# Attention and spectral layers in one program: exponents and scores take five banks in turn, the first projections are stored from other buffers, and a chunk's stack is loaded by eight transfers instead of twelve

## The chip, the cores and the metric

One core of a Trainium2 chip runs the whole program. The metric is the device time of one execution in microseconds (us). TensorE (PE in the profile) multiplies matrices and writes to PSUM, which has eight banks of 512 float32 a partition; its weight loads have a row of their own, PEld. VectorE is DVE, ScalarE is ACT, GpSimd is POOL, and SP issues most transfers between the chip's memory (SBUF) and HBM. Each engine works through its own list of instructions in order, and waits where an instruction needs what another engine has not yet done.

## The reference

Four layers in a row, A, B, A, B, over x of 2048 positions by 576. Each adds to x what it makes of its normalised x:

```python
qkv = (x @ wqkv).reshape(B, S, 3, H, Dh)          # H = 32 heads of Dh = 18
scores = einsum("bhqd,bhkd->bhqk", q, k) * Dh ** -0.5
mask = (i - j >= 0) & (i - j < 256)                # a sliding window
o = softmax(where(mask, scores, -1e9)) @ v         # layer A
x = x + o @ wo
x = x + irfft2(rfft2(_layernorm(x)) * W)           # layer B
```

## The kernel before

The program runs `layer_a` and `layer_b` twice. Only the second half of `layer_a` is touched: the attention.

*Numbers in two parts.* A matmul takes operands in a short float format, so most operands are split into a high part and a low part, and a product is summed from three. `proj(i, c, tag, halves)` makes unit i (128 of the 1152 rows of q and k) for chunk c (512 positions) in 14 such steps. With `halves` each step is two matmuls of 64 rows that may run at once, into two banks; ScalarE copies one bank (L747), VectorE adds the other (L748), GpSimd makes the high part and the low part (L749, L750), and SP stores both to `qk_d` in HBM (L755). The result stands in a tile `sg`, of which there are two. Units 0 and 1 come ahead of the loop, and units 2 to 8 are spread over it by the table `goal`, step by step.

*Stacks.* For a group n of four heads, `stack_load(n, c)` brings q and k of a chunk from `qk_d` to SBUF: head pairs `hp` lie in partitions from 64 * hp on, and there three slots of 18 rows hold high or low parts, so that one matmul sums the three products. Each slot is one transfer: 2 tensors x 2 head pairs x 3 slots, 12 a chunk.

*The loop.* t runs from -10 to 129. Block x of 128 positions belongs to group x // 16. In turn t the program does, for pair 0 and then for pair 1: two exponent blocks `exps(t, pair, hp)` (a matmul E on TensorE, L822, then the exponent on ScalarE, L823, into a tile `P`, of which there are five), then two score maxima `score_max(t + 10, pair, hp)` (a matmul S, L790, and the masked maximum on VectorE, L792, into `m`), and after pair 0 the products with v, `pv(t - 2)` (U, L842). Then come the projection steps of the turn; in turns before t = 2 the first half of them stands after pair 0. So the maxima run ten turns ahead of the exponents; for t < 0 there are only maxima and projections, and from t = 118 on only exponents. Every fourth turn `m_rows` turns four blocks' maxima around (tpm, L798) and sends them as a row of q (L805), and `norm` turns results around (tpo, L852) and divides them (L855, L857). GpSimd masks the exponents (L825, L828).

*Banks.* U has one of eight, `pj` two. `S` has three, which maxima, `m_rows` and `norm` use in turn. `E` has two, which the four exponent blocks of a turn use in turn (and units of i = 2 with odd c before the loop reaches t = 0). In the last turns some exponents use banks of S. A matmul into a bank waits until the reader of its former content is done: ScalarE for exponents, VectorE for maxima.

The order on every engine is the order of the code: nothing is rearranged by a scheduler. The numbers in names such as `E37_1` are the turn and the head.

## Time and profile before

| | us |
|---|---|
| median of 3 runs | 1580.11 (1578.26 to 1594.03) |
| the profiled execution | 1586.13 |
| its span, first to last instruction | 1584.4 |
| TensorE busy | 1452.4 (92%) |
| VectorE busy | 944.0 (60%) |
| ScalarE busy | 823.8 (52%) |
| GpSimd busy | 753.4 (48%) |
| mean granted TensorE clock | 0.964 of full speed |

The attention loop of the first layer A runs from about 107 us (first S) to 505 us, with its first exponent (t = 0) at 139 us; that of the second from about 900 to 1300 us. In rows of waits the columns are the engine and line that waited, what released it, the total of us, how many times, and the longest. In rows of groups, a line, engine and operation come first, then "busy, mean ns of one", and behind the bar the idle time ahead of it and what ended it. A matmul's recorded time runs from its start to its modelled end, so matmuls overlap in the rows, and the distance of two starts says more than one duration.

### The profile page before, as it was taken

How to read it: one execution, taken by the hardware profiler on the slowest of the kernel's cores; microseconds unless marked ns; L12 is line 12 of the kernel's file. 1: busy time of each engine (PE TensorE's matmuls, PEld its weight loads, DVE VectorE, ACT ScalarE, POOL GpSimd, SP SyncE). 2: the span in 40 equal slices, each digit the busy share in tenths (PEclk: the TensorE clock that was granted, in tenths of full speed). 3: DMA queues.
4: the chain of work that ended last, by engine and by line, in shares of the span. 5: the costliest groups of instructions: out<-in, count | busy, mean ns of one | idle time of the engine just before them, and what ended most of it. 6: DMA issues, size and time to landing. Idle time of an engine off the chain costs nothing. (4 is left out here: it accounts for less than half of the span.)

```text
span 1584.4 us, 35203 instructions
## 1 busy us (share of the span) xinstructions
PE 1452.4 (92%) x12312; PEld 1077.3 (68%) x12312; DVE 944.0 (60%) x3083; ACT 823.8 (52%) x1900; POOL 753.4 (48%) x1240
## 2 busy tenths in 40 slices
PE   7998999999999899877879989999999998997787
PEld 7976666666655799536779766666666557995376
DVE  4337777777764555444543377777777645554445
ACT  5524666666667344224445246666666673442244
POOL 2185556555545333144611855555555463332445
PEclk9999999999988999988989999999999899999889
DMA  6656455554444366666474564544444443657664
GB/s 205 177 182 207 142 156 183 152 165 145 151 128 123 118 196 200 220 195 209 142 229 118 181 202 146 155 150 145 139 130 149 128 129 118 196 194 230 191 206 139
DMA packets 196414, 264.43 MB, mean 167 GB/s; under 512 B 87182, under 2 KB 109326, under 8 KB 195406
## 3 DMA queue, kind: packets, MB, share of 16 engines
q1 hardware_dynamic: 184494, 243.28, 49.6%
q10 hardware_dynamic: 10976, 15.59, 3.0%
q0 software_dynamic: 768, 3.31, 0.8%
q8 instruction: 99, 1.62, 0.4%
q14 instruction: 77, 0.63, 0.1%
HBM read 163.46 MB, written 100.91 MB: 167 GB/s over the span
## 5 line engine op out<-in xcount | busy, mean ns | idle before, releaser
L792 DVE CUSTOM_DVE_ANT_0 jk<-S,mask 128x384 bf16<-128x384 f32 (+2 forms) x1024 | 499.5, 529 | 144.3 <-PE S L790 130.8
L823 ACT ACTIVATE P<-E 128x384 f32<-128x384 f32 (+2 forms) x1024 | 427.8, 473 | 204.3 <-PE E L822 176.6
L825 POOL TENSOR_SCALAR_AFFINE_SELECT P<-P 128x512 f32<-128x512 f32 x256 | 163.0, 637 | 311.0 <-ACT P L823 292.0
L822 PE MATMUL E<-qs,ks 64*128 64x384 f32 (+2 forms) x1024 | 285.2, 429 | 10.2 <-ACT P L823 8.2
L790 PE MATMUL S<-ks,qs 63*128 63x384 f32 (+2 forms) x1024 | 250.7, 362 | 9.4 <-DVE m L792 9.0
L822 PEld LDWEIGHTS E<-qs,ks 64*128 64x128 f32 x1024 | 138.3, 186 | 136.4 <-ACT P L823 80.7
L842 PE MATMUL U<-P,vq 128*19 128x128 f32 (+1 forms) x3840 | 208.2, 336 | 0.3
L741 PE MATMUL pj<-xh,wqh 64*128 64x512 f32 (+1 forms) x640 | 172.5, 404 | 5.5 <-ACT sg L747 3.4
L790 PEld LDWEIGHTS S<-ks,qs 63*128 63x128 f32 x1024 | 141.9, 190 | 27.0 <-DVE m L792 20.5
L842 PEld LDWEIGHTS U<-P,vq 128*19 128x19 f32 x3840 | 91.2, 99 | 100.5 <-issue 40.8
L828 POOL TENSOR_SCALAR_AFFINE_SELECT P<-P 128x512 f32<-128x512 f32 x224 | 142.7, 637 | 0.0
L741 PE MATMUL pj<-xl,wqh 64*128 64x512 f32 (+1 forms) x512 | 136.1, 395 | 0.0
L741 PE MATMUL pj<-xh,wql 64*128 64x512 f32 (+1 forms) x640 | 129.2, 398 | 1.4 <-POOL wql L431 1.4
L527 PE MATMUL ops<-oroom 128*128 128x288 f32 x784 | 112.4, 299 | 4.4 <-DVE oroom L510 3.0
L527 PEld LDWEIGHTS ops<-oroom 128*128 128x128 f32 x784 | 105.2, 188 | 6.2 <-DVE oroom L510 4.0
L741 PEld LDWEIGHTS pj<-xh,wqh 64*128 64x128 f32 (+1 forms) x640 | 95.0, 187 | 11.2 <-ACT sg L747 3.9
L171 POOL TENSOR_TENSOR eo<-xn 128x287 f32<-128x287 f32 x32 | 26.1, 817 | 150.4 <-ACT xn L169 150.4
L741 PEld LDWEIGHTS pj<-xh,wql 64*128 64x128 f32 (+1 forms) x640 | 84.4, 190 | 6.9 <-POOL wql L431 2.0
L792 DVE DVE_READ_ACCUMULATOR2_ANT m<- 128x1 f32 x1024 | 85.0, 83 | 0.0
L199 PE MATMUL pf<-dc,et 128*128 128x290 f32 x384 | 72.3, 313 | 9.7 <-DVE et L190 6.5
L741 PEld LDWEIGHTS pj<-xl,wqh 64*128 64x128 f32 (+1 forms) x512 | 78.6, 187 | 3.0
L750 POOL TENSOR_TENSOR sg<-sg 128x512 fp32r<-128x512 f32 x56 | 72.2, 1289 | 4.7
(179 smaller groups left out, 2567.0 us busy)
## 6 DMA issues: line engine op xcount, KB each, us to landing
qk_d<-sg SPq DMA_DIRECT2D x56, 512.0 KB
qs<-qk_d SPq DMA_DIRECT2D x384, 72.0 KB
ks<-qk_d SPq DMA_DIRECT2D x384, 72.0 KB
v_d<-vt SPq DMA_DIRECT2D x32, 304.0 KB
vq<-v_d SPq DMA_DIRECT2D x16, 608.0 KB
yd<-ye SPq DMA_DIRECT2D x32, 290.0 KB
wt<-in_w SPq DMA_DIRECT2D x16, 580.0 KB
x<-ofree SPq DMA_DIRECT2D x32, 288.0 KB
```

What stands on the lines that cost most here:

```text
L171: P.tensor_add(eo[:, 0, 1:288], xn[:, 1:288], xn[:, 575:288:-1])
L199: T.matmul(o, et[:, c, si], m(5 * c + mi), start=q == 0, stop=False)
L527: self.nc.tensor.matmul(self.ps[u][n][:, 0:288], x, self.w[p][:, wk * D + n * 288:wk * D + n * 288 + 288], start=first and i == 0, stop=la ...
L741: T.matmul(ps, w[r, wk], xT(xk, cs)[r], start=s == 0, stop=s == len(ks) - 1)
L750: P.tensor_sub(sg[:, 1], su, sg[:, 0].bitcast(F32))
L790: T.matmul(ps[:, 0:N], q[b:b + 63, pair, i * 128:i * 128 + 128], k[b:b + 63, pair, lo:hi], start=True, stop=True)
L792: V.tensor_tensor_reduce(out=jk[:, 0:N], in0=ps[:, 0:N], in1=mask[:, 384 - N:384], scale=1.0, scalar=-3e38, op0=ALU.add, op1=ALU.max, accu ...
L822: T.matmul(ps[:, 0:nq], k[b:b + 64, pair, j * 128:j * 128 + 128], q[b:b + 64, pair, j * 128:j * 128 + nq], start=True, stop=True)
L823: A.activation(p[:, hl_, 0:nq], ps[:, 0:nq], AF.Exp, scale=SC)
L825: P.affine_select(out=p[:, :, 0:128], in_=p[:, :, 0:128], pattern=[[0, 4], [1, 128]], compare_op=ALU.is_ge, fill=0.0, base=0, channel_mult ...
L828: P.affine_select(out=p[:, :, 256:384], in_=p[:, :, 256:384], pattern=[[0, 4], [-1, 128]], compare_op=ALU.is_gt, fill=0.0, base=0, channel ...
L842: T.matmul(U[32 * h:32 * h + 19, (q0 % 4) * 128:(q0 % 4) * 128 + 128 * (q1 - q0)], vts[n][:, j, h], pt[n, j][:, h, (q0 - j) * 128:(q1 - j) ...
```

## The change

It has four parts.

1. `bank(name)` hands out five banks in a fixed order, S S E E S, one place further with each call once t is 0 or more; all users of S and E in the loop call it: maxima, exponents, `m_rows`, `norm`. For t < 0 it always gives a bank of S. What was a separate rule for the last turns' exponents goes.
2. A unit with `halves` that ends while t < 0 puts its result into a buffer of `P` (five, unused before t = 0), not into one of the two `sg`.
3. For such a unit ScalarE's copy stays in place, but VectorE's sum, GpSimd's split and the store are kept in a list `later`, and done after the next two maxima.
4. `qk_cols` lays the columns of the weights so that the two heads of a pair alternate row by row in `qk_d`. A slot of 18 partitions by 2 heads is then one run of 36 rows, and one transfer can bring two neighbouring slots: 8 transfers a chunk in place of 12, with the same bytes.

On TensorE the order of instructions is the same, and what some wait for is another. Turn 37, first before, then after (E37_0 to E37_3 are exponents, S47 the maxima of block 47, U the products with v; Activation is ScalarE, Pool is GpSimd):

```order
L822 MATMUL E37_0_3688<-qs0_1034,ks0_1035 128x384 [waits Activation_49]
L822 MATMUL E37_2_3691<-qs0_1034,ks0_1035 128x384 [waits Activation_49]
L790 MATMUL S47_0_0_3694<-ks0_1035,qs0_1034 128x384 [waits DVE_49]
L790 MATMUL S47_0_1_3698<-ks0_1035,qs0_1034 128x384 [waits DVE_49]
L842 MATMUL U_1038<-P2_2_3520,vq2_2748 19x256 [waits Pool_49]
L842 MATMUL U_1038<-P2_2_3520,vq2_2748 19x256 x3
L842 MATMUL U_1038<-P2_3_3570,vq2_2748 19x128 [waits Pool_49]
L842 MATMUL U_1038<-P2_3_3570,vq2_2748 19x128 x3
L822 MATMUL E37_1_3712<-qs0_1034,ks0_1035 128x384 [waits Activation_49]
L822 MATMUL E37_3_3715<-qs0_1034,ks0_1035 128x384 [waits Activation_49]
L790 MATMUL S47_1_0_3720<-ks0_1035,qs0_1034 128x384 [waits DVE_49]
L790 MATMUL S47_1_1_3724<-ks0_1035,qs0_1034 128x384 [waits DVE_49]
```

```order
L831 MATMUL E37_0_3628<-qs0_1034,ks0_1035 128x384 [waits DVE_49]
L831 MATMUL E37_2_3631<-qs0_1034,ks0_1035 128x384 [waits Activation_49]
L799 MATMUL S47_0_0_3634<-ks0_1035,qs0_1034 128x384 [waits Activation_49]
L799 MATMUL S47_0_1_3638<-ks0_1035,qs0_1034 128x384 [waits DVE_49]
L851 MATMUL U_1038<-P2_2_3464,vq2_2704 19x256 [waits Pool_49]
L851 MATMUL U_1038<-P2_2_3464,vq2_2704 19x256 x3
L851 MATMUL U_1038<-P2_3_3514,vq2_2704 19x128 [waits Pool_49]
L851 MATMUL U_1038<-P2_3_3514,vq2_2704 19x128 x3
L831 MATMUL E37_1_3652<-qs0_1034,ks0_1035 128x384 [waits DVE_49]
L831 MATMUL E37_3_3655<-qs0_1034,ks0_1035 128x384 [waits Activation_49]
L799 MATMUL S47_1_0_3660<-ks0_1035,qs0_1034 128x384 [waits Activation_49]
L799 MATMUL S47_1_1_3664<-ks0_1035,qs0_1034 128x384 [waits DVE_49]
```

The first of each pair of exponents now waits for a maximum on VectorE, and the first of each pair of scores for an exponent on ScalarE.

On VectorE, ahead of t = 0, the sum of a unit moves behind two maxima. Unit 2, chunk 1, in the turn of block 3, before and after (`jk` with `m` is a maximum, the row of `m` alone its second half, `sg2_1` the sum, `jk4` the next block):

```order
L792 ISA jk3_0_1_1393,m0_0_1268<-S3_0_1_1391,mask_1026 128x384
L792 ISA m0_0_1268 128x1
L748 TENSOR_TENSOR sg2_1_1403<-sg2_1_1403,pj2_1_1_1338 128x512
L792 ISA jk3_1_0_1411,m0_0_1268<-S3_1_0_1409,mask_1026 128x384
L792 ISA m0_0_1268 128x1
L792 ISA jk3_1_1_1415,m0_0_1268<-S3_1_1_1413,mask_1026 128x384
```

```order
L801 ISA jk3_0_1_1377,m0_0_1256<-S3_0_1_1375,mask_1026 128x384
L801 ISA m0_0_1256 128x1
L801 ISA jk3_1_0_1391,m0_0_1256<-S3_1_0_1389,mask_1026 128x384
L801 ISA m0_0_1256 128x1
L801 ISA jk3_1_1_1395,m0_0_1256<-S3_1_1_1393,mask_1026 128x384
L801 ISA m0_0_1256 128x1
L751 TENSOR_TENSOR sg2_1_1387<-sg2_1_1387,pj2_1_1_1322 128x512
```

Five units in each layer A move so; on ScalarE and GpSimd the order stays. On SP each chunk's twelve loads become eight, and the first unit's store, which stood between two chunks' loads, comes after them.

```diff
@@ qk_cols
             for hp in range(2):
-                for pair in range(2):
-                    h = head_of(n, hp, pair)
-                    c += [qk * D + h * DH + d for d in range(DH)]
+                c += [qk * D + head_of(n, hp, pair) * DH + d for d in range(DH) for pair in range(2)]
@@ proj
-                        sg = wp.tile([128, 2, 512], F32R, tag="sg", name=f"sg{i}_{c}", bufs=2)
-                        if halves:
-                            su = sg[:, 1].bitcast(F32)
-                            A.copy(su, ps[0])
-                            V.tensor_add(su, su, ps[1])
-                            P.tensor_copy(sg[:, 0], su)
-                            P.tensor_sub(sg[:, 1], su, sg[:, 0].bitcast(F32))
+                        if halves and t < 0:
+                            sg = wp.tile([128, 4, 384], F32, tag="P", name=f"sg{i}_{c}", bufs=5).rearrange("p a b -> p (a b)")[:, 0:1024].bitcast(F32R).rearrange("p (a t) -> p a t", a=2)
                         else:
-                            A.copy(sg[:, 0], ps[0])
-                            V.tensor_sub(sg[:, 1], ps[0], sg[:, 0].bitcast(F32))
-
-                        (nc.scalar if i < 2 else nc.sync).dma_start(qk_d[:, 128 * i:128 * i + 128, cs].rearrange("a r t -> r a t").bitcast(F32), sg.bitcast(F32))
+                            sg = wp.tile([128, 2, 512], F32R, tag="sg", name=f"sg{i}_{c}", bufs=2)
+                        su = sg[:, 1].bitcast(F32) if halves else ps[0]
+                        A.copy(su if halves else sg[:, 0], ps[0])
+
+                        def rest():
+                            if halves:
+                                V.tensor_add(su, su, ps[1])
+                                P.tensor_copy(sg[:, 0], su)
+                            (P if halves else V).tensor_sub(sg[:, 1], su, sg[:, 0].bitcast(F32))
+                            (nc.scalar if i < 2 else nc.sync).dma_start(qk_d[:, 128 * i:128 * i + 128, cs].rearrange("a r t -> r a t").bitcast(F32), sg.bitcast(F32))
+                        if halves and t < 0:
+                            later.append(rest)
+                        else:
+                            rest()
+            turns, later = [0], []
+
+            def bank(name):
+                turns[0] += t >= 0
+                return pp.tile([128, 512], F32, name=name, **(dict(tag="E", bufs=2) if turns[0] % 5 > 2 else dict(tag="S", bufs=3)))
@@ stack_load
-                for which, t, parts in ((0, q, (0, 0, 1)), (1, k, (0, 1, 0))):
+                for which, t, parts in ((0, q, ((0, slice(0, 1)), (1, slice(0, 2)))), (1, k, ((0, slice(0, 2)), (2, slice(0, 1))))):
                     for hp in range(2):
                         r0 = 144 * n + 72 * which + 36 * hp
-                        for slot, part in enumerate(parts):
+                        for slot, part in parts:
                             b = 64 * hp + 18 * slot
-                            nc.sync.dma_start(t[b:b + 18, :, cs].bitcast(F32),
-                                              qk_d[part, r0:r0 + 36, cs].rearrange("(f d) t -> d f t", f=2).bitcast(F32))
+                            nc.sync.dma_start(t[b:b + 18 * (part.stop - part.start), :, cs].bitcast(F32), qk_d[part, r0:r0 + 36, cs].bitcast(F32))
@@ score_max, m_rows, exps, norm
-                ps = pp.tile([128, 512], F32, tag="S", name=f"S{x}_{pair}_{hp}", bufs=3)
+                ps = bank(f"S{x}_{pair}_{hp}")
-                tp = pp.tile([128, 4, 128], F32, tag="S", name=f"tpm{n}_{c}", bufs=3)
+                tp = bank(f"tpm{n}_{c}").rearrange("p (a t) -> p a t", a=4)
-                ps = pp.tile([128, 512], F32, name=f"E{x}_{hl_}", **(dict(tag="S", bufs=3) if pair and NX - LEAD <= x < NX - 4 else dict(tag="E", bufs=2)))
+                ps = bank(f"E{x}_{hl_}")
-                tp = pp.tile([128, 4, 128], F32, tag="S", name=f"tpo{n}_{c}", bufs=3)
+                tp = bank(f"tpo{n}_{c}").rearrange("p (a t) -> p a t", a=4)
@@ the loop
                         if t + LEAD < NX:
                             score_max(t + LEAD, pair, hp)
+                    while later:
+                        later.pop()()
                     if pair == 0 and 0 <= t - 2 < NX:
                         pv(t - 2)
```

## The prediction

> **What bounds the kernel now.** I read the page's first part, then stretches of the span with their granted clock, then the list of waits, and at last the timeline of one turn.
>
> ```profile
> span 1584.4 us, 35203 instructions
> PE 1452.4 (92%) x12312; PEld 1077.3 (68%) x12312; DVE 944.0 (60%) x3083; ACT 823.8 (52%) x1900; POOL 753.4 (48%) x1240
> 160.00:440.00 280.00, 279.00 (x2861) 176.05 (x2857) 213.84 (x823) 185.70 (x449) 159.09 (x236) 1.00 0.51 155
> 487.00:505.00 18.00, 16.61 (x179) 8.51 (x179) 4.86 (x18) 15.73 (x38) 11.18 (x17) 1.00 0.39 114
> 126.50:130.00 3.50, 3.50 (x20) 3.44 (x18) 1.91 (x9) 0.00 (x0) 0.97 (x1) 0.51 0.86 281
> 464.50:485.00 20.50, 19.98 (x128) 10.27 (x121) 12.01 (x47) 10.77 (x28) 9.31 (x12) 0.50 0.05 9
> 918.40:921.90 3.50, 3.50 (x22) 3.50 (x20) 2.02 (x10) 0.00 (x0) 1.10 (x1) 0.51 0.88 279
> 1256.40:1266.60 10.20, 10.20 (x74) 5.18 (x74) 6.20 (x24) 3.87 (x12) 3.90 (x5) 0.50 0.04 7
> L825 POOL TENSOR_SCALAR_AFFINE_SELECT P<-P 128x512 f32<-128x512 f32 x94 | 59.8, 636 | 114.2 <-ACT P L823 106.5 <-DMA ks<-qk_d 5.5 <-DMA o_d<-o 2.1
> ```
>
> The stretches are from the two attention loops (columns: window, length, PE, PEld, DVE, ACT, POOL busy, granted clock, DMA share, GB/s); the last row, for 160 to 440 us, has one L825 a turn. TensorE bounds the loop: 279 of 280 us, VectorE 76%, ScalarE 66%, and 94 turns in 280 us make 2.98 us a turn. But a busy TensorE is not one without waits: a matmul whose partner is late stays open. The waits show it. Below are rows for the whole run, for 160 to 440, for 960 to 1225 (the second layer's loop), and for both loops' ends (440 to 487, 487 to 505, 1225 to 1282, 1282 to 1300):
>
> ```profile
> PEld E L822 <- ACT P L823: 80.7, 315, 1.0
> PEld E L822 <- ACT P L823: 22.7, 100, 0.5
> PEld E L822 <- ACT P L823: 21.5, 95, 0.5
> PEld E L822 <- ACT P L823: 8.9, 25, 0.9
> PEld E L822 <- ACT P L823: 4.4, 14, 0.9
> PEld E L822 <- ACT P L823: 11.3, 33, 1.0
> PEld E L822 <- ACT P L823: 3.7, 13, 0.9
> ```
>
> The exponents' matmuls E wait 80.7 us for ScalarE to empty one of only two banks, all over both loops. The maxima's three banks hold TensorE far less in the loop (3.5 us of S behind m in the same window of 280 us):
>
> ```profile
> PEld S L790 <- DVE m L792: 3.5, 13, 0.5
> ```
>
> **One turn.** The timeline from 304.13 us (start, length, engine, line; the waits in brackets):
>
> ```profile
> 304.13 0.34 PE L790 MATMUL S<-ks,qs 63*128 63x384 f32 x2
> ...
> 305.18 0.51 PE L822 MATMUL E<-qs,ks 64*128 64x384 f32 x2
> ...
> 305.65 0.88 ACT L823 ACTIVATE P<-E 128x384 f32<-128x384 f32 x2 [0.46 <-PE E L822]
> ...
> 305.87 0.47 PE L741 MATMUL pj<-xh,wql 64*128 64x512 f32 x2
> 306.20 0.18 PEld L822 LDWEIGHTS E<-qs,ks 64*128 64x128 f32 x1 [0.30 <-ACT P L823]
> ...
> 306.32 0.55 DVE L792 CUSTOM_DVE_ANT_0 jk<-S,mask 128x384 bf16<-128x384 f32 x1
> ...
> 306.58 0.18 PEld L822 LDWEIGHTS E<-qs,ks 64*128 64x128 f32 x1 [0.20 <-ACT P L823]
> ...
> 306.58 0.62 PE L790 MATMUL S<-ks,qs 63*128 63x384 f32 x2
> ...
> 307.13 0.85 PE L842 MATMUL U<-P,vq 128*19 128x256 f32 x16
> ```
>
> Two heads' matmuls run at once where both may start: a pair of S took 0.34 us. In the next turn the first E waits until 306.20, the second until 306.58, just after ScalarE's pair ends (305.65 + 0.88 = 306.53). The first S then runs beside the late E, the second alone: 0.62 for two. So 0.50 us of recorded waiting costs 0.62 - 0.34 = 0.28 us.
>
> **The change, part 1: five banks in turn.** The order on TensorE stays; each matmul now waits for the bank used five matmuls earlier. Followed through a turn of E E S S U E E S S, the bank of the last E goes to the next turn's first S, where it went to the second E; the first E of a pair waits for a maximum and the second for an exponent one place older. In the turn above both E would start when the projection lets them, and the pair of S at 306.58, when the same exponents end, together instead of 0.28 us apart. A wait of up to 0.28 us vanishes and a longer one loses about that. I scale all such waits by 0.28 / 0.50 = 0.56. Not scaled are the 4.4 + 3.7 = 8.1 us of the last stretches, where ScalarE is busy 15.73 of 18 us and would only wait elsewhere: (80.7 - 8.1) x 0.56 = **40.7 us**. Bounds: nothing, if S takes over every wait, and 72.6 us if each recorded microsecond is worth one. I take 40.7, since it is what the turn shows.
>
> What is late next: the second S and the fourth S wait for maxima as before, and now the first and third E do too. The last maximum of the turn above ends at 306.32 + 0.55 = 306.87; the E that takes its bank opens the next turn's second pair, behind U. U starts at 307.13 today, would start 0.28 earlier, and takes 0.85: 307.7, less what the next matmul overlaps with it. Some 0.7 us is left. Behind a waiting E stand that turn's S, U and projection, and POOL's masks wait for its exponents.
>
> **Part 2: first units in the exponents' buffers, sums later.** Each layer's first five units of proj with t < 0. Today in layer one (two stretches of the timeline):
>
> ```profile
> 123.22 0.33 PE L790 MATMUL S<-ks,qs 63*128 63x384 f32 x1
> ...
> 124.13 0.59 ACT L747 COPY sg<-pj 128x512 f32<-128x512 f32 x1 [2.83 <-DMA qk_d<-sg]
> 124.75 0.69 DVE L748 TENSOR_TENSOR sg<-sg,pj 128x512 f32<-128x512 f32 x1 [2.29 <-ACT sg L747]
> 125.35 0.55 DVE L792 CUSTOM_DVE_ANT_0 jk<-S,mask 128x384 bf16<-128x384 f32 x1
> ...
> 125.96 0.44 PE L790 MATMUL S<-ks,qs 63*128 63x384 f32 x1 [2.42 <-DVE m L792]
> ```
>
> A store holds ScalarE's copy, the copy holds VectorE's sum, the sum stands ahead of the maxima, and TensorE stands still for 2.42 us. With five buffers the copy needs no store, and with the sum behind two maxima these don't wait for it. For 100 to 145 and for 898 to 945 us, TensorE's own idle time:
>
> ```profile
> PE S L790 <- DVE m L792: 3.8, 4, 2.4
> PE pj L741 <- ACT sg L747: 1.5, 1, 1.5
> ...
> PE S L790 <- DVE m L792: 4.6, 4, 3.0
> PE pj L741 <- ACT sg L747: 1.9, 1, 1.9
> ```
>
> Of 3.8 + 4.6 = 8.4 I take 7.8: 0.3 in each layer is left, by estimate, for waits that no sum stands ahead of. The pj waits stay: there the fifth unit's banks are wanted at once by the sixth, and its sum now stands behind two maxima of 0.55 us, 1.1 us that eat most of the copy's gain. That adds a wait: behind that pj stand the rest of its projection and the next S and E. It is priced at 0; its ends are -2.2 (1.1 us more in each layer) and +3.4 (both waits gone). The half clock of 126.5 to 130 came right behind the 2.42 us; layer two has one as long at 918.4. Running 3.4 us at half rate loses 1.7; I count one of the two. Part 2 gives 7.8 + 1.7 = **9.5 us**, between 7.8 - 2.2 = 5.6 and 8.4 + 3.4 + 3.4 = 15.2.
>
> The Trainium skill, page "TensorE: Matmul & The Clock Gate", section "Part 1: The HAM clock gate (the "warmup" mystery)", says the clock halves after an idle window of about 3.4 us. By that, 2.42 us need not halve it and the 1.7 would not be this change's; the sum would be 1537.6. The row of 0.51 behind that gap speaks against it.
>
> **Part 3: eight loads a chunk.** The bytes stay; four issues of twelve go. Six cost SP 2.75 us, so a chunk's four are worth 1.83 us of SP's time:
>
> ```profile
> 116.63 2.75 SPq L769 DMA_DIRECT2D ks<-qk_d  x6
> ...
> PE E L822 <- DMA qs<-mt: 0.3, 1, 0.3
> ```
>
> The second row, from 898 to 945, is the only wait of TensorE for a transfer there. The loads are issued ten turns (some 29 us) ahead of their scores: **0**. Were that cover gone, 4 chunks x 8 groups x 2 layers x 1.83 = 117 us could go or, if a load of two parts landed later than its two predecessors, come; neither has a trace. The first unit's store moves behind eight loads in SP's queue; nobody needs its data before the loads four turns later.
>
> **The sum.** The profiled execution took 1586.13 us, its span 1584.4 and 1.7 around it. 1586.1 - 40.7 - 9.5 = 1535.9, 3.2% less. That execution lies 6 us above the median of 1580.11, from which the same sum gives 1530. I say **1535**.
>
> **The rivals.**
> - *Half of it* (0.20). S takes more of the waits, since exponents of one turn still set the next turn, and the pj wait grows: 25 us, 1561. For it: a pair's latency, E to the end of its exponents, is 306.53 - 305.18 = 1.35 us and no bank shortens it. Against it: S stands a pair later than E.
> - *More* (0.13). All 72.6 us go, 9.5 more, and the half clock at the loops' ends (20.5 + 10.2 us, which loses at most half) goes too: 1586 - 72.6 - 9.5 - 15 = 1489. For it: those stretches follow waits of E of up to 1.0 us. Against it: ScalarE and TensorE are near balance there, so gaps stay.
> - *It doesn't do what it says* (0.05). E merely waits under another name, PE stays at 2.98 us a turn, and part 2's gain is lost at the sixth unit: 1575 to 1585.
> - *Slower: E behind maxima* (0.07). VectorE works in order, and between maxima stand a sum, or a reciprocal and a product:
>
> ```profile
> L748 DVE TENSOR_TENSOR sg<-sg,pj 128x512 f32<-128x512 f32 x20 | 13.7, 687 | 6.2 <-issue 4.8 <-PE E L822 0.9 <-POOL P L825 0.3
> L855 DVE RECIPROCAL rc<-tpo 128x16 f32<-128x16 f32 x24 | 6.2, 258 | 10.2 <-PE tpo L852 10.2
> L857 DVE TENSOR_TENSOR o<-tpo,rc 128x288 f32<-128x288 f32 x24 | 11.0, 457 | 0.8
> ```
>
>   If VectorE runs further behind TensorE than the 0.7 us above, each such turn holds E and with it ScalarE for 0.69 or 0.72 us: 20 x 0.69 + 24 x 0.72 = 31 us in 280, 33 in a layer's 300, and 66 for two. With nothing gained by part 1: 1586 - 9.5 + 66 = 1643; with half of 40.7 gained, 1622. VectorE's 76% speaks against it.
> - *Slower: the clock* (0.04). If the cycling of banks left gaps that halve the clock in the loops for as much of the time as at their ends (30.7 of 140 us), 0.22 x 545 = 120 us would run at half rate and lose 60: 1586 - 9.5 + 60 = 1637. A granted 1.00 in the loop, where banks cycle already, speaks against it. The Trainium skill, in the same page's section "A second HAM failure mode: psum-queue depth-cycling", tells of a kernel whose cycling through banks idled TensorE often enough for that; the loop here does not bear it out.
>
> **How the numbers follow.** The forecast has 0.51, with 1520 to 1552. About 1% is what a measurement of this kernel tells from no change, 1564 to 1596. Faster: 0.51 + 0.13 + three quarters of the 0.20, 0.79. Within 1%: a quarter of the 0.20 and 0.05, 0.10. Slower: 0.11. The range 1505 to 1570 holds the forecast, nearly all of *half of it* and half of *more*; the bounds beyond (1489, and 1586 with nothing gained) are left out with 2 in 10.
>
> **What would show it.** Right: E's wait behind P falls from 80.7 to under 40, S behind P is new with about a quarter of that, 94 turns take some 267 us; no wait of an L747 copy for a store before t = 0; SP issues 512 loads of q and k. Wrong: rows of E behind m of 20 us and more, a clock under 1.00 inside the loops, PE idle before pj between 130 and 140 us grown past 3 us, or E waiting for loads of ks or qs.

## The result, and the profile after

The changed kernel takes 1951.07 us (median of four executions) against 1582.29 us for the kernel before in the same session: a ratio of **1.231 (95% interval 1.222 to 1.239)**. Three of the four took 1947.26 to 1951.41 us; the fourth took 3111.51 us, in a slow state that the ratio leaves out. Forecast were 1535 us, with 1505 to 1570 as the range. The profiled execution took 1951.41 us. The page of after, first part, clock and transfers:

```profile
span 1949.7 us, 35129 instructions
PE 1532.5 (79%) x12312; PEld 1125.4 (58%) x12312; DVE 947.2 (49%) x3083; ACT 824.3 (42%) x1900; POOL 753.6 (39%) x1240
...
PEclk9986878888887699997989868888988878999979
DMA  7534333333332155675464333333333322556654
```

TensorE, which had been busy for 92% of the span, now is for 79%, with the same 12312 matmuls; in both loops the granted clock (PEclk) falls mostly to 7 and 8 tenths, and the transfers' share mostly to 3 tenths. The same 260 us of the first loop, before and then after (columns: window, length, PE, PEld, DVE, ACT, POOL busy, granted clock, DMA share, GB/s):

```profile
160.00:420.00 260.00, 259.16 (x2659) 163.43 (x2655) 197.76 (x763) 172.79 (x417) 150.29 (x223) 1.00 0.52 157
```

```profile
160.00:420.00 260.00, 188.73 (x1728) 118.20 (x1728) 130.33 (x504) 116.19 (x278) 99.83 (x146) 0.82 0.36 113
```

A third fewer matmuls fit in, at a clock of 0.82. Who is waited for, over the whole run of after (TensorE's waits, then those of SP's queue):

```profile
PE E L831 <- DMA qs<-mt: 256.4, 44, 12.3
PEld E L831 <- ACT P L832: 34.7, 73, 9.2
SPq L814 <- DMA ks<-qk_d: 114.7, 60, 3.3
SPq L779 <- DMA ks<-qk_d: 94.3, 48, 4.0
```

The second row is what part 1 was to do: E's wait behind ScalarE was 80.7 us and is 34.7. But the first row, which came to 0.3 us before, is 256.4: E waits 44 times, up to 12.3 us, for the rows of maxima that `m_rows` sends. And SP, which issues both these rows (L814) and the stack loads (L779), is itself held by loads of ks. The trace shows how: in the loop the transfers take eight semaphores in turn, and no issue ends before the transfer eight places ahead of it, which had the same one, has landed. So at most eight are under way, and one that lands late stops the queue. One chunk of the loop in SP's queue, before and then after (start, length, queue, line, transfer, count):

```profile
242.11 2.46 SPq L805 DMA_DIRECT2D qs<-mt  x4
...
246.25 2.55 SPq L769 DMA_DIRECT2D qs<-qk_d  x6
248.85 3.04 SPq L769 DMA_DIRECT2D ks<-qk_d  x6
```

```profile
238.02 4.94 SPq L814 DMA_DIRECT2D qs<-mt  x4
245.11 3.16 SPq L779 DMA_DIRECT2D qs<-qk_d  x4
248.31 4.20 SPq L779 DMA_DIRECT2D ks<-qk_d  x4
252.62 0.50 SPq L871 DMA_DIRECT2D o_d<-o  x1
253.22 5.13 SPq L814 DMA_DIRECT2D qs<-mt  x4
```

Eight issues take 7.4 us where twelve took 5.6, and mt's four take twice as long, since the first of them alone holds SP for 2.93 of the 4.94 us, until a load has landed. A load of two parts lands a median of 7.1 us (q) and 11.3 us (k) after the start of its issue, where a load of before took 3.2 and 3.7; mt's own rows take 7.1 us and took 2.1. In the stretches of after in which nearly nothing but loads of two parts is in flight, the DMA engines look like this; behind it is a stretch of before with its loads:

```profile
107.50:110.50 3.00, 0.69 (x4) 0.23 (x2) 0.69 (x1) 0.59 (x1) 2.88 (x4) 1.00 0.13 52
113.00:114.50 1.50, 0.00 (x0) 0.00 (x0) 0.00 (x0) 0.00 (x0) 1.46 (x2) 0.50 0.12 42
```

```profile
117.00:119.00 2.00, 1.40 (x14) 1.03 (x12) 1.67 (x6) 0.92 (x2) 1.86 (x4) 1.00 0.53 183
```

0.12 to 0.13 of 16 engines is two engines, with 42 to 52 GB/s; before, it was 0.53 and 183 GB/s. A chunk has four loads of two parts, 4 x 147 kB; at 42 to 52 GB/s they last 11.3 to 14.0 us. A chunk of before lasts 11.9 us (80 turns of the loop, by the first E of each), so these loads alone nearly fill two engines, or more than fill them. A chunk of after lasts 17.0 us in layer one and 16.8 in layer two.

### The profile page after: what moved, and what is told of

Same layout as the page of the kernel before. It is cut to its first block, busy times and chain, and to the rows that moved or that the text cites. A ratio compares the mean times of both kernels' runs of the same rounds, so it can differ in the third digit from the quotient of the medians.

```text
span 1949.7 us, 35129 instructions
## 1 busy us (share of the span) xinstructions
PE 1532.5 (79%) x12312; PEld 1125.4 (58%) x12312; DVE 947.2 (49%) x3083; ACT 824.3 (42%) x1900; POOL 753.6 (39%) x1240
## 5 line engine op out<-in xcount | busy, mean ns | idle before, releaser
L831 PE MATMUL E<-qs,ks 64*128 64x384 f32 (+2 forms) x1024 | 274.2, 469 | 274.1 <-DMA qs<-mt 256.4
L799 PE MATMUL S<-ks,qs 63*128 63x384 f32 (+2 forms) x1024 | 250.3, 405 | 28.9 <-DMA ks<-qk_d 17.9
L851 PE MATMUL U<-P,vq 128*19 128x128 f32 (+1 forms) x3840 | 234.2, 369 | 1.0 <-POOL P L837 1.0
L739 PE MATMUL pj<-xh,wqh 64*128 64x512 f32 (+1 forms) x640 | 180.3, 451 | 4.3 <-DVE sg L751 2.6
L799 PEld LDWEIGHTS S<-ks,qs 63*128 63x128 f32 x1024 | 142.8, 221 | 56.9 <-issue 21.8
L851 PEld LDWEIGHTS U<-P,vq 128*19 128x19 f32 x3840 | 97.0, 106 | 120.5 <-issue 67.7
L739 PE MATMUL pj<-xh,wql 64*128 64x512 f32 (+1 forms) x640 | 133.5, 433 | 0.0
```

The source lines that it names most:

```text
L739: T.matmul(ps, w[r, wk], xT(xk, cs)[r], start=s == 0, stop=s == len(ks) - 1)
L799: T.matmul(ps[:, 0:N], q[b:b + 63, pair, i * 128:i * 128 + 128], k[b:b + 63, pair, lo:hi], start=True, stop=True)
L831: T.matmul(ps[:, 0:nq], k[b:b + 64, pair, j * 128:j * 128 + 128], q[b:b + 64, pair, j * 128:j * 128 + nq], start=True, stop=True)
L851: T.matmul(U[32 * h:32 * h + 19, (q0 % 4) * 128:(q0 % 4) * 128 + 128 * (q1 - q0)], vts[n][:, j, h], pt[n, j][:, h, (q0 - j) * 128:(q1 - j) ...
```

## The experiments

Sixteen kernels, each timed against the kernel before on the same chip. None leaves out anything that the reference computes. "B+S" is short for the run with the banks and the late sums and without the loads.

### Which part costs it

**The loads alone** (e1): the kernel before with the alternating columns and the eight loads of the change.

```diff
-                for pair in range(2):
-                    h = head_of(n, hp, pair)
-                    c += [qk * D + h * DH + d for d in range(DH)]
+                c += [qk * D + head_of(n, hp, pair) * DH + d for d in range(DH) for pair in range(2)]
...
-                            nc.sync.dma_start(t[b:b + 18, :, cs].bitcast(F32),
-                                              qk_d[part, r0:r0 + 36, cs].rearrange("(f d) t -> d f t", f=2).bitcast(F32))
+                            nc.sync.dma_start(t[b:b + 18 * (part.stop - part.start), :, cs].bitcast(F32), qk_d[part, r0:r0 + 36, cs].bitcast(F32))
```

> The kernel before, with the columns of a head pair alternating and the eight loads a chunk, and nothing else of the change: banks, first units and sums are as before. Theory A (the loads): a load of two parts has as its source 2 parts of 36 rows of 512, and in the trace of after a stretch with only such loads in flight (113.0 to 114.5 us) shows a DMA share of 0.12 of 16 engines and 42 GB/s, two engines' worth, where the old loads of one part reach 0.53 and 183 GB/s (117 to 119 us of before). Then this part alone makes the kernel slow, and the time is 1900 to 2000 us: E waits for qs behind mt's transfers by some 250 us, as in after, and the clock falls. Theory B (the banks or the late sums make it slow, the loads' waits only follow): within 1% of before, 1566 to 1598. The prediction on record had 0 for this part.

Measured: 1953.22 us, ratio 1.235 (1.230 to 1.239), as slow as the whole change; E waits 212.1 us for mt. Theory A holds, B falls.

**All but the loads** (e2, B+S): the changed kernel with the old columns and twelve loads, that is, e1's edit undone.

> The changed kernel with the old columns and the old twelve loads a chunk: the cycling banks, the first units in the exponents' buffers and the late sums stay. Theory A (the loads): 1520 to 1552 us, which is the prediction's 40.7 + 9.5 us without its part 3; E waits for mt's transfers by under 5 us a loop, and E's wait behind P stays under 40 us. Theory B (the banks or the late sums): 1900 us or more. If A holds and the time lies between 1552 and 1575, part 1 gains half of what was put down for it.

Measured: 1565.27 us, ratio 0.989 (0.985 to 0.992). So the loads cost 386 us (1951.07 - 1565.27); the rest gains, but 19 us (1584.60 - 1565.27) rather than 50, in the half-gain band of the expectation. Here E's waits are as follows:

```profile
PEld E L834 <- ACT P L835: 24.0, 80, 0.7
PEld S L802 <- ACT P L835: 17.4, 88, 0.2
PE E L834 <- DMA qs<-mt: 11.2, 3, 6.4
PEld E L834 <- DVE m L804: 11.0, 50, 0.5
PE E L834 <- ACT P L835: 4.7, 16, 0.4
```

11.2 us in three waits for mt are a little more than the 5 us a loop that were allowed for. They return below.

**The banks alone** (e5): `bank()` and its four users, with the old sums and loads.

```diff
-                ps = pp.tile([128, 512], F32, tag="S", name=f"S{x}_{pair}_{hp}", bufs=3)
+                ps = bank(f"S{x}_{pair}_{hp}")
...
-                ps = pp.tile([128, 512], F32, name=f"E{x}_{hl_}", **(dict(tag="S", bufs=3) if pair and NX - LEAD <= x < NX - 4 else dict(tag="E", bufs=2)))
+                ps = bank(f"E{x}_{hl_}")
```

> The kernel before with the five banks in turn and nothing else. The prediction on record has 40.7 us for it, a ratio of 0.974. In the run with the banks and the late sums, turns 4 to 104 of the two layers' loops took 574.9 us and not 591.0, and from turn 104 to the last exponents' scores 115.6 and not 130.8: by that, the banks alone are worth 31 us, a ratio of 0.980, some 1553 us beside 1584.6. Rival: the banks gain only together with the late sums, and alone stay within 1% of before.

Measured: 1568.17 us, ratio 0.988 (0.982 to 0.994), some 19 us. The banks gain by themselves, as much as together with the sums, but less than either figure.

**The sums alone** (e6): units with `halves` that end while t < 0 go into the buffers of P, with their sums behind two maxima; banks and loads are old.

```diff
+                        if halves and t < 0:
+                            sg = wp.tile([128, 4, 384], F32, tag="P", name=f"sg{i}_{c}", bufs=5).rearrange("p a b -> p (a b)")[:, 0:1024].bitcast(F32R).rearrange("p (a t) -> p a t", a=2)
...
+                        if halves and t < 0:
+                            later.append(rest)
```

> The kernel before with the first units in the exponents' buffers and the sums behind the next maxima, the old banks and the old loads. The prediction on record has 9.5 us for it, a ratio of 0.994. Theory G (given back): from the first S to turn 0 some 12 us of the two layers go, as in the run with both parts, and E's waits for mt's transfers of 4 to 7 us in each layer bring them back: within 0.3% of before. Rival H: the waits for mt come of the banks, and alone this part keeps 9 to 12 us.

Measured: 1584.03 us beside 1586.84, ratio 0.998 (0.996 to 1.001): theory G. Its trace has one wait of E for mt in each layer, 4.7 and 6.7 us, without any new banks, so H falls.

The stages of both layers together show where each gains (us; turn t begins with its first E):

| | first S to turn 0 | turns 0 to 4 | 4 to 104 | 104 to last E | all else |
|---|---|---|---|---|---|
| before | 65.6 | 21.0 | 591.0 | 130.8 | 776.0 |
| after | 104.0 | 52.6 | 847.4 | 160.0 | 785.7 |
| banks alone (e5) | 69.8 | 21.5 | 575.0 | 122.7 | 781.4 |
| sums alone (e6) | 52.9 | 36.0 | 590.3 | 127.8 | 776.4 |
| B+S (e2) | 53.2 | 34.4 | 574.8 | 115.7 | 781.9 |
| B+S, loads behind mt (e13) | 52.8 | 21.8 | 580.2 | 124.9 | 777.8 |

### What it is in the loads

**New rows, but twelve loads of one part** (e3): against the changed kernel,

```diff
-                            nc.sync.dma_start(t[b:b + 18 * (part.stop - part.start), :, cs].bitcast(F32), qk_d[part, r0:r0 + 36, cs].bitcast(F32))
+                            nc.sync.dma_start(t[b:b + 18, :, cs].bitcast(F32), qk_d[part, r0:r0 + 36, cs].rearrange("(d f) t -> d f t", f=2).bitcast(F32))
```

> The changed kernel with its alternating columns, but twelve loads of one part each in place of eight: each load takes 36 alternating rows as 18 pairs, so its source is 18 by 2 by 512. Theory A (the loads of two parts): within 1% of the kernel with the old columns and twelve loads, some 1520 to 1552 us. Theory C (the alternating rows, which make each store's and load's rows lie otherwise): 1900 us or more. It parts the layout from the shape of the load.

Measured: 1719.06 us, ratio 1.086 (1.082 to 1.089). Neither theory had this: 154 us over B+S, with the same twelve transfers of as many rows to the same places. SP's queue shows the difference:

```profile
237.43 4.82 SPq L779 DMA_DIRECT2D qs<-qk_d  x6
242.30 4.64 SPq L779 DMA_DIRECT2D ks<-qk_d  x6
247.04 0.40 SPq L754 DMA_DIRECT2D qk_d<-sg  x1
247.54 2.57 SPq L814 DMA_DIRECT2D qs<-mt  x4
```

A load holds the queue for 0.74 us where it held it for 0.32 (median of 768 issues each). In before, the source is 18 by 2 rows with two separate steps, like the destination; here the 36 rows follow each other, and the transfer as built has them as one run of 36 against 18 by 2.

**Eight loads, the parts side by side** (e4): the source of a load of two parts is one run of 72 rows.

```diff
-    qk_d = dram.tile([2, 1152, S], F32R, name="qk_d")
+    qk_d = dram.tile([32, 2, 36, S], F32R, name="qk_d")
...
-                            nc.sync.dma_start(t[b:b + 18 * (part.stop - part.start), :, cs].bitcast(F32), qk_d[part, r0:r0 + 36, cs].bitcast(F32))
+                            nc.sync.dma_start(t[b:b + 18 * (part.stop - part.start), :, cs].bitcast(F32), qk_d[r0 // 36, part, :, cs].bitcast(F32))
```

> The changed kernel with its eight loads a chunk, but with qk_d laid out so that the two parts of 36 rows lie side by side: the source of a load of two parts is one run of 72 rows of 512 and not 2 by 36. Bytes, count and destination of the loads stay. The price is that a unit's store becomes 4 to 5 transfers. Theory A (the source's outermost size of 2 confines the load to two engines): the loads spread, a stretch with only loads in flight shows a DMA share above 0.3, and the time is 1520 to 1570 us. Theory D (fewer and larger loads are slow as such, for instance because mt's rows queue behind 144 KB): E still waits some 250 us for qs behind mt and the time stays at 1900 us or more. The Trainium skill, page "DMA: Bandwidth & Descriptors", section "Why a DMA increments its semaphore by 16 and not by 1", says that a transfer is split over the largest number of engines up to 16 that divides the outermost size of both sides; that is theory A.

Measured: 1644.72 us, ratio 1.040 (1.036 to 1.045). With the same eight loads, bytes and destinations 306 us are gone, and in stretches filled with these loads the engines' share is 0.47:

```profile
242.70:246.00 3.30, 3.26 (x35) 2.15 (x34) 2.97 (x12) 3.19 (x8) 2.52 (x4) 1.00 0.47 115
246.00:249.00 3.00, 3.00 (x37) 1.87 (x34) 2.55 (x10) 1.57 (x5) 2.37 (x4) 1.00 0.47 148
```

The spread, not number or size, is most of what made after slow; D falls. By the rule of the Trainium skill that the expectation names, 72 against 36 gives 12 engines. 0.47 of 16 is 7.5, a mean over all that was in flight, and shows only that it is more than two. But the traces also record each increment of a transfer's semaphore: a load of two parts makes 3 in after and 13 here, and a load of one part 10 in all three kernels, each one more than the 2, 12 and 9 that the rule gives. But the time missed its 1520 to 1570: each load, of 36 rows or of 72, holds SP for 0.76 to 0.79 us here, and of the 80 us that it lies above B+S 28 arise ahead of turn 0 (80.9 for 53.2), where a unit's store is four or five transfers, and 54 in turns 4 to 104, where SP pauses hardly at all: from 160 to 420 us its pauses of more than 0.2 us come to 6.7 us, and in before to 70.9.

**Six slow issues of twelve** (e7): only q's rows alternate.

```diff
-                                              qk_d[part, r0:r0 + 36, cs].rearrange("(f d) t -> d f t", f=2).bitcast(F32))
+                                              qk_d[part, r0:r0 + 36, cs].rearrange("(f d) t -> d f t" if which else "(d f) t -> d f t", f=2).bitcast(F32))
```

> The run with the banks and the sums (twelve loads a chunk), but q's six loads have their rows as 36 in a row, as in the run with the new rows and twelve loads, where one such load held SP's queue for 0.737 us and not 0.321; k's six are as before. Theory I (SP's queue, which issues in order, is the bound): a chunk costs SP 6 x 0.78 + 6 x 0.37 for the loads, 4 x 0.62 for mt and 0.9 for two stores, 10.3 us, less than the 11.5 us of four turns; with all twelve slow it was 12.8. So nearly all of the 154 us come back: within 1.5% of the run with the banks and the sums, 1560 to 1590 us. Theory J (each slow load costs E by landing late, whatever else is in the queue): half of the 154 us stays, some 1640.

Measured: 1611.43 us, ratio 1.016 (1.010 to 1.022); 46 us over B+S, between I (up to 25) and J (77). A steady chunk costs little more than before (12.2 and 11.9 us for B+S's 11.6), as I has it, but E waits 29.3 us for mt.

**Half of the two-part loads** (e12): q in four loads, k in its old six.

```diff
+                            if which:
+                                nc.sync.dma_start(t[b:b + 18, :, cs].bitcast(F32),
+                                                  qk_d[part.start, r0:r0 + 36, cs].rearrange("(f d) t -> d f t", f=2).bitcast(F32))
+                            else:
+                                nc.sync.dma_start(t[b:b + 18 * (part.stop - part.start), :, cs].bitcast(F32), qk_d[part, r0:r0 + 36, cs].bitcast(F32))
```

> The run with the banks and the sums, but q's rows alternate and come in four loads a chunk, two of them of two parts, while k's six loads stay as they were. Two engines then hold 2 x 72 x 84 ns / 2 = 6 us a chunk, half of what after has, and SP's queue some 8.6 us. Theory P (a queue: nothing is lost until a chunk's transfers take longer than its four turns of 11.5 us): 1565 to 1620 us. Theory Q (each load of two parts costs E a time of its own): half of the 386 us between that run and after, some 1760 us.

Measured: 1773.7 us, ratio 1.120 (1.115 to 1.124). Q's number came true and P's did not: a queue that is not yet full costs as well. The trace shows why: SP stands still until loads of q have landed, since no more than eight transfers are under way.

```profile
SPq L783 <- DMA qs<-qk_d: 126.7, 64, 4.2
SPq L821 <- DMA qs<-qk_d: 91.2, 34, 3.3
```

L783 are k's loads, L821 mt's rows. So there is something that can't wait even for half a chunk's loads.

### What can't wait: mt

In the loop of before, ScalarE makes a chunk's rows of maxima (`mt`) a median of 8.1 us ahead of the E that first needs them (chunks other than a group's first). Their issue takes SP 2.5 us, and they have landed a median of 3.3 us ahead of that E. So a wait of a few us in the queue, or a landing as much later, reaches E, though the stack loads have ten turns. In B+S the first such place:

```profile
131.41 0.26 ACT L812 ACTIVATE mt<-tpm 16x128 fp32r<-16x128 f32 x1
...
132.43 3.26 SPq L781 DMA_DIRECT2D qs<-qk_d  x6
136.40 3.93 SPq L781 DMA_DIRECT2D ks<-qk_d  x6
...
140.92 2.59 SPq L817 DMA_DIRECT2D qs<-mt  x4
...
143.83 1.00 PE L834 MATMUL E<-qs,ks 64*128 64x384 f32 x2 [4.48 <-DMA qs<-mt]
```

In before the same row of mt was made at 137.07 and issued at 140.43:

```profile
131.22 3.20 SPq L769 DMA_DIRECT2D qs<-qk_d  x6
135.17 3.07 SPq L769 DMA_DIRECT2D ks<-qk_d  x6
137.07 0.26 ACT L800 ACTIVATE mt<-tpm 16x128 fp32r<-16x128 f32 x1
...
140.43 2.65 SPq L805 DMA_DIRECT2D qs<-mt  x4
```

The late sums bring mt 5.7 us forward; its issue stays, behind twelve loads.

**All loads three turns later** (e8).

```diff
-                n, c = divmod(t + 20, NT)
+                n, c = divmod(t + 17, NT)
```

> The run with the banks and the sums, but every stack's loads are issued three turns later, so that those of the second head group stand behind mt's transfers of the first group's second chunk in SP's queue and not ahead of them. Theory K (order in SP's queue): in the run before, mt was ready at 131.7 us and issued at 140.9, behind twelve loads; so E's waits for mt of 4.5 and 6.4 us go, and with them some 11 us: 1548 to 1558 us. Theory L (the transfers of that stretch together are the bound, at a DMA share of 0.65 to 0.78): E waits as long, for mt or for ks, and the time stays at 1560 to 1570 us.

Measured: 1593.94 us, ratio 1.005 (1.003 to 1.008), and so outside both. Turns 0 to 4 of layer one went from 16.6 to 10.5 us, as K had it, but turns 4 to 104 of both layers took 30 us more (605.1 for 574.8), and E's waits for mt grew to 27.7 us in seven pieces. One of them:

```profile
180.00 0.27 ACT L812 ACTIVATE mt<-tpm 16x128 fp32r<-16x128 f32 x1 [1.41 <-PE tpm L810]
...
180.63 2.49 SPq L781 DMA_DIRECT2D qs<-qk_d  x6
183.16 2.65 SPq L781 DMA_DIRECT2D ks<-qk_d  x6
186.69 2.45 SPq L817 DMA_DIRECT2D qs<-mt  x4
...
189.52 0.99 PE L834 MATMUL E<-qs,ks 64*128 64x384 f32 x2 [3.81 <-DMA qs<-mt]
```

Here mt was made before the loads were issued, and still stands behind them. By the code that is where `m_rows` is put off by a turn because a unit ends; the later loads then come ahead of it.

**One stack later** (e9): only the first load of the second group moves, from turn -4 to -1.

```diff
-                if c % 4 == 0 and 0 < n < NQ:
+                if c % 4 == 0 and 0 < n < NQ and t != -4:
                     stack_load(n, c // 4)
+                if t == -1:
+                    stack_load(1, 0)
```

> The run with the banks and the sums, but of all stack loads only one is moved: the first of the second head group, from turn -4 to turn -1, behind mt of the first group's second chunk. With all loads moved, turn 0 to 4 of layer one took 10.5 us and not 16.6, and 6 to 8 us each were lost later, between turns 16 and 32, 64 and 80 and 104 and 112. Theory K (a chunk's mt waits in SP's queue for the twelve loads ahead of it): the first gain stays and the later losses don't come: 1550 to 1560 us. Theory L (the transfers together are the bound): the wait moves to another place of the first turns, 1560 to 1570.

Measured: 1563.57 us, ratio 0.989 (0.985 to 0.993), B+S's own. Turns 0 to 4 of both layers take 12 us less (22.5 for 34.4), and turns 4 to 104 take 15 more: mt of the next chunk, made at 142.1 us, is issued at 151.1 behind its twelve loads. That is L's number, by K's mechanism one chunk on.

**ScalarE issues mt** (e10 with B+S, e11 with the changed kernel).

```diff
-                        nc.sync.dma_start(q[b:b + 1, pair, c * 512:c * 512 + 512].rearrange("a (t q) -> a t q", t=4).bitcast(F32),
+                        nc.scalar.dma_start(q[b:b + 1, pair, c * 512:c * 512 + 512].rearrange("a (t q) -> a t q", t=4).bitcast(F32),
```

> The run with the banks and the sums, but ScalarE issues mt's four transfers of a chunk and not SP, so that no load stands ahead of them. Theory K: E's waits for mt (11.2 us) go. The price is ScalarE's time, four issues of some 0.58 us a chunk, 147 us over 64 chunks; ScalarE is busy for 204 of the loop's 300 us. If two thirds of that stay hidden, E's waits for exponents grow by some 50 us in all and the time is about 1600 us; if all of it is hidden, 1550 to 1558.

> The changed kernel, with its eight loads, but ScalarE issues mt's transfers. In after a chunk takes 16.7 us of the loop. Theory M (two bounds, one behind the other: mt waits in SP's queue for the loads, and the loads themselves hold two engines for 4 x 72 x 84 ns / 2 = 12.1 us a chunk, by the 84 ns of a packet of 2 KB, with some 1.3 us for the other four): the chunk falls to 13 to 14 us, and 56 chunks give some 1740 to 1800 us. Theory N (only the order in SP's queue counts, since the loads come ten turns ahead): 1570 to 1640 us. Theory O (mt's own transfers wait for the same engines, whoever issues them): above 1900 us, as before.

Measured: 1813.05 us (1.145; 1.140 to 1.150) and 1956.38 us (1.238; 1.233 to 1.242). The first is far above its 1600, since ScalarE's own work stops (e10):

```profile
250.06 2.44 ACTq L817 DMA_DIRECT2D qs<-mt  x4
252.60 1.64 ACT L835 ACTIVATE P<-E 128x384 f32<-128x384 f32 x4 [2.57 <-DMA qs<-mt]
```

ScalarE makes no exponent for 2.6 us, E waits for it, and a chunk takes 15.5 us (15.0 in layer two). So these two runs settle little: e11's number is that of theory O, but ScalarE's stop is in it. Nor does ScalarE's queue free mt of the loads, since its transfers take the same eight semaphores: in e11 mt's four issues last a median of 4.4 us, in e10 2.4.

**Loads behind mt** (e13 with B+S, e14 with the changed kernel, e15 with e3's twelve loads, e16 with e4's eight): no code of the loop calls `stack_load` any more but this.

```diff
-                n, c = divmod(t + 20, NT)
-                if c % 4 == 0 and 0 < n < NQ:
-                    stack_load(n, c // 4)
...
                     f(n, c)
                     due.pop(0)
+                    if f is m_rows and 4 <= 4 * n + c + 3 < 4 * NQ:
+                        stack_load(*divmod(4 * n + c + 3, 4))
```

> The run with the banks and the sums, but a stack's loads are issued directly behind mt's transfers of a chunk (that of three chunks earlier), so that no load ever stands ahead of mt in SP's queue. In that run mt's rows were issued a median of 0.36 us after ScalarE had made them, at most 2.82, and E needs them 7.8 us after; at the loops' starts, where a wait of 9 us stood between, E waited 4.5 and 6.4 us. Theory K (order in SP's queue): those two waits go and none comes in the loop: 1548 to 1558 us. Theory L (the transfers of the first turns together are the bound): the waits move, as when one stack was moved: 1560 to 1570.

Measured: 1555.84 us, ratio **0.979 (0.976 to 0.983)**, better than both kernels. E's waits for mt fall from 11.2 to 1.7 us, and turns 0 to 4 take 21.8 and not 34.4: K, as to the waits. In the traces as much comes back, 5.4 us in turns 4 to 104 and 9.2 behind them. Behind turn 104 the granted clock is 0.92 and 0.89 in the two layers here, and was 1.00 and 0.97 in B+S's profiled execution; the two spans are 2.5 us apart. So that this order is the better one rests on the medians, and how much of the 9 us between them is its own is not shown.

> The changed kernel with its eight loads, issued directly behind mt's transfers. Theory R (in after, mt's rows are late because they stand behind loads in SP's queue): mt is issued at once, the loads have eight turns (23 us) until their first reader, and the time is 1570 to 1640 us. Theory S (the engines that a load of two parts uses are the bound): a chunk has 4 x 72 packets of 84 ns on two engines, 12.1 us, and some 1.3 us of the other loads, 13.4 together, more than four turns of 11.5; 56 chunks lose at least 1.9 us each, 106 us, and more where mt's rows land behind that backlog: 1670 to 1900 us.

Measured: 1905.37 us, ratio 1.200 (1.196 to 1.205), 5 us above S's upper end. A chunk still takes 16.9 us, and E waits nearly as long as in after:

```profile
PE E L831 <- DMA qs<-mt: 209.0, 44, 8.9
```

So in after the order in SP's queue is worth 46 us of 386. The rest goes with the engines: only spreading the loads (e4) took most of it away. Here too SP waits for loads of ks to land, 80.4 us at mt's issues and 87.1 at other loads, and mt's rows land a median of 6.7 us after the start of their issue (1.8 in e13).

> The changed kernel with its new rows and twelve loads of one part, issued directly behind mt's transfers. One such load holds SP's queue for 0.737 us, so a chunk costs SP 12 x 0.78 + 4 x 0.62 + 0.9 = 12.8 us, more than four turns of 11.5. Theory U (SP's issue time is a bound of its own): 56 x 1.3 to 1.8 us more than the run with the banks and the sums, 1630 to 1670 us. Theory V (only mt's place behind the slow loads counts): 1550 to 1590 us.

Measured: 1713.56 us, ratio 1.079 (1.074 to 1.084): U in kind, larger in size. SP issues without a pause, a chunk in 13.4 us:

```profile
242.50 2.78 SPq L814 DMA_DIRECT2D qs<-mt  x4
245.32 4.75 SPq L779 DMA_DIRECT2D qs<-qk_d  x6
250.11 4.64 SPq L779 DMA_DIRECT2D ks<-qk_d  x6
254.85 0.40 SPq L871 DMA_DIRECT2D o_d<-o  x1
255.36 0.44 SPq L754 DMA_DIRECT2D qk_d<-sg  x1
255.89 2.66 SPq L814 DMA_DIRECT2D qs<-mt  x4
```

2.78 + 4.75 + 4.64 + 0.40 + 0.44 = 13.0, and the rest is the steps between them. From 160 to 420 us SP's pauses of more than 0.2 us come to 8.6 us. A queue that hardly pauses is the bound, whatever stands first in it.

> The kernel with qk_d's parts side by side and eight loads a chunk, issued directly behind mt's transfers. SP's queue has 8 x 0.80 for the loads, 4 x 0.62 for mt, 4 x 0.46 for a store's pieces and 0.4, 11.1 us a chunk, just under four turns. If the 80 us that it lost to the run with the banks and the sums were mt's wait behind loads (a median of 3.34 us there), most of them come back: 1560 to 1600 us. If SP's queue is full in any case, 1620 to 1650.

Measured: 1645.14 us, ratio 1.036 (1.032 to 1.040), as e4; the upper case. SP's queue, with 0.76 us a load and a store in pieces, is near its limit in any order, and mt still waits a median of 3.0 us for its issue. Of the 80 us above B+S, by the traces, 27 lie ahead of turn 0 and 60 in turns 4 to 104.

## Why the prediction was wrong

**The step that failed is part 3, priced at 0**: "The bytes stay; four issues of twelve go", and "The loads are issued ten turns (some 29 us) ahead of their scores". Alone it costs 369 us (1953.22 - 1584.60). Three things were wrong in it.

- *The bytes stay, but not the engines.* A source of 2 parts by 36 rows ran at 42 to 52 GB/s on two engines, where a stretch with loads of 18 by 2 reached 183 GB/s. Four such loads need 11.3 to 14.0 us of a chunk that had 11.9, and a chunk takes 17.0. The dimension of parts comes first in the source, which the diff shows. The Trainium skill, page "DMA: Bandwidth & Descriptors", section "Why a DMA increments its semaphore by 16 and not by 1", states the rule behind it: a transfer runs on the largest number of engines up to 16 that divides the outermost size of both sides, here 2 and 36. The prediction passed over it; the 0.12 to 0.13 of 16 engines and the 3 increments of such a load agree with its 2.
- *An issue is not a fixed price.* 1.83 us were to go from SP's time, four times the 0.46 of a row. But the issues that stay grew from 0.32 to 0.74 us as soon as the source was one run of rows. Twelve such loads alone cost 154 us.
- *The cover was that of the wrong reader.* Ten turns hold for the scores that read the loads. Behind the loads, in the same queue, comes mt, which E needs 8.1 us after it is made; and with at most eight transfers under way, a load that lands late holds every issue behind it. Which engines mt's rows use no trace tells, but they too took 7.1 us to land and not 2.1. The cover of the loads themselves nearly held: S waited 21.0 us for them in all of after. The row "PE E <- DMA qs<-mt: 0.3" was read as proof that transfers don't matter; it said only that mt's rows were in time, by a median of 3.3 us.

The prediction did put down that 117 us "could go or, if a load of two parts landed later than its two predecessors, come; neither has a trace". That was the question to answer, and it was left at zero with no bound taken into the range; and its 117 us were SP's issue time, not engines. None of its rivals had the loads. *Slower: the clock* was seen in the rows (0.82 in the loop), but as a consequence: e1 has it (0.872 over its span, after 0.868) without any new bank. From B+S to after the span grows by 389.7 us: 245.2 are E's waits for mt (256.4 - 11.2), and 107.6 are TensorE's longer busy time for the same matmuls, at a granted clock of 0.868 for 0.969 (1532.5 - 1424.9).

**Part 1, 40.7 us**: the waits moved as forecast, but the term was too large. From turn 4 to the last E the banks alone give 24.1 us (591.0 + 130.8 - 575.0 - 122.7), B+S 31.3. E's wait behind P fell as forecast, from 80.7 to 24.0 us in B+S (under 40). But S behind P came to 17.4, where a quarter of E's was put down, and E behind maxima, which was to stay within 0.7 us of slack, to 11.0. In before E also waits as a matmul:

```profile
PE E L822 <- ACT P L823: 8.2, 21, 0.8
```

80.7 + 8.2 = 88.9 before; in B+S 24.0 + 17.4 + 11.0 + 4.7 = 57.1; 31.8 less. That this is near the gain of 31.3 is in part luck: 15.1 of the 31.3 lie behind turn 104, where the granted clock of the two layers was 0.85 and 0.90 in before's profiled execution and 1.00 and 0.97 in B+S's. What the banks have to do with that clock is not shown; the banks alone have 0.84 and 0.97 there and gain 8.1. In turns 4 to 104, at full clock in both, the gain is 16.2 us (16.0 for the banks alone), where before had 50.8 us of E's waits behind P, and S behind maxima, which the sum above leaves out, grew from 7.3 to 14.4. The factor was thus 0.32 there, and 0.43 of the 72.6 us over all (0.33 for the banks alone), not 0.56: the case *half of it*. Turns of the loop take 2.89 us (a chunk's 11.57 by four), so 94 take 272 us, not 267. E behind maxima is real, but never as the 66 us of that rival.

**Part 2, 9.5 us**: the wait of 2.42 us and its like went, and more than forecast: 12.7 us from the first S to turn 0 (e6). 15.0 came back between turns 0 and 4, since mt stood behind twelve loads. What failed is the cover again: "nobody needs its data before the loads four turns later" asked for the store's reader, not for what else waits in SP's queue. The wait at pj was rightly priced near 0 (3.4 us before, 2.6 in B+S). With the loads behind mt the gain stays, and banks, sums and this order give 33.5 us (1589.35 - 1555.84) of the 50.2 forecast.

The 1.7 us for the half clock hold up: in B+S, where the gap of 2.42 us is gone, the same stretch has full clock, where before had 0.51 from 126.5 on.

```profile
124.00:130.00 6.00, 5.95 (x54) 5.18 (x50) 5.87 (x23) 0.59 (x1) 3.30 (x4) 1.00 0.74 254
```

Of the signs that the prediction named for "wrong", a clock under 1.00 inside the loops came, and so did waits for transfers, though E's were for mt's rows and only S waited for the loads of ks (17.9 us) and qs (3.1 us); of those for "right", E behind P under 40 us and 512 loads came too. The copies of L747 wait for no store ahead of t = 0 in B+S; in after they do (11.4 us in layer one), since the stores are late themselves. Each part did what it says to the waits that it was made for, but the loads cost twenty times what the others gained together (386 us for 19).

## What to carry to other kernels

Before two transfers are merged, look at four prices: the outermost sizes of source and destination, which went with 2 engines or more here, the time that its issue holds the queue, the time until it lands, since only eight were under way at once here, and what stands behind it. A cover is that of the tightest transfer in the same queue, not that of the data moved: put the short, urgent one first and the long ones behind it, as e13 does.

## What was not expected of the hardware

- Two loads of 36 rows to the same places hold SP's queue for 0.32 us where both sides are 18 by 2, and for 0.74 us where the source is one run of 36 (e3); with 72 rows against 36 by 2 it is 0.77 to 0.79 (e4). Length does not set it. Why the shapes do was not found out.
- At most eight transfers of SP and ScalarE together are under way in the traces of before, after, e11 and e14; from 160 to 420 us it was eight for 17.6 us in before and for 64.5 in after.
- Four transfers issued by ScalarE held its next instruction for 2.57 us, and cost the loop 3.5 to 3.9 us a chunk (15.0 and 15.5 for 11.6), more than the hold. Waits of TensorE are followed by half clock, which may be the rest. A wait of 4.48 us for mt in B+S, for example, is followed by this:

```profile
143.20:150.00 6.80, 6.17 (x37) 3.98 (x37) 2.80 (x11) 2.88 (x7) 1.22 (x2) 0.55 0.57 171
```
